# First batch of an attention and feed-forward kernel: two difference buffers and 512-wide exponentials in the key phases, one unit of 256 for the last 64 query tokens of four head pairs

## The chip, the core and the metric

The kernel runs on one core of a Trainium2 chip. The core has five engines with instruction queues of their own: TensorE (PE in the profile; its weight loads are shown apart as PEld), VectorE (DVE), ScalarE (ACT), GpSimd (POOL) and SyncE (SP, which issues the DMAs here). Each engine works its queue in order; semaphores tie the queues together. The metric is the time of one execution on the device in microseconds, and the median of several runs is compared. Less is better.

## The reference

Linear attention over 8 batches of 8 heads and 576 tokens, with a feature map of 2 x 128 exponentials, and then one feed-forward layer over all 4608 tokens:

```python
def phi(x):
    proj = np.einsum('bhsd,df->bhsf', x, w_phi)
    proj = proj - np.max(np.abs(proj), axis=-1, keepdims=True)
    return np.concatenate([np.exp(proj), np.exp(-proj)], axis=-1)
q_p, k_p = (phi(q), phi(k))
kv = np.einsum('bhsf,bhsd->bhfd', k_p, v)
z = np.sum(k_p, axis=2)
num = np.einsum('bhsf,bhfd->bhsd', q_p, kv)
den = np.einsum('bhsf,bhf->bhs', q_p, z)[..., None] + 1e-06
attn = num / den
x = attn.transpose(0, 2, 1, 3).reshape(4608, 512)
h = x @ w_in                      # 512 -> 2048
out = np.maximum(0.01 * h, h) @ w_out   # 2048 -> 512
```

## The kernel before

**Tiling.** Two heads share the 128 partitions, so a batch is four *pairs*; pairs 0 to 31 are worked in order, and pairs 0 to 3 are the first batch. The attention output of two batches at a time lies in `ring` (128 x 2 x 4 x 576): batch b writes half b mod 2. The feed-forward part works on 18 *blocks* of 256 tokens. Block 0 and block 1 lie within batch 0; block 2 has tokens 512 to 767, so it needs batch 0's last 64 tokens and also all four pairs of batch 1 (pairs 4 to 7). A block has 16 steps: `layer1(i, ft)` is 12 matmuls of 256 columns (L552, L553, L555), `layer2(i, ft)` 6 matmuls of 512 columns (L572 to L574), which follow three steps behind. Most products are split: a value is rounded to a shorter format (the cast, `copy_`, L67 on ACT, L69 on DVE), the rest is the difference (`tt_`, L72), and three matmuls make one product.

**Weights.** `load_weights` prepares 32 tiles (16 of `w_in`, 16 of `w_out`, in turns). Each is loaded by SP (L153) into one of two places in `ring[:, 1]`, the half that batch 1 will need later, and then takes on DVE L159, L160, L161, L164 and the difference of L72, on ACT L158, L163 and the cast of L67. Here `ql` and `kvl` are the names of its scratch tiles.

**The first batch.** It has its own code, since no feed-forward work is there yet to lie beside it. `first_k_phase(i)` makes the key side of pair i: three groups (128, 128 and 64 partitions) of projections (`proj`, three matmuls each), per group an absolute maximum (L417), a difference `pm` (L419, always the buffer `pmk`), then exponentials of `pm` and of `-pm` (L428, L429), 256 wide, two for each 128 tokens, and two matmuls into `kvp` (L431). At the end `kvp` is copied to `kvs`, transposed and stored as `kvh`. Phases 0 and 1 run together, step by step in turns, then 2 and 3. Odd phases take other buffers than even ones, some of them parts of `f2`, `f3`, `fr1`, `fr4`: four tiles whose space the last quarter of the weights takes over later (tag `late`). `first_q_phase(u)` makes the query side of all four pairs for the tokens of one unit: unit 0 has 256, unit 1 has 256, unit 2 has 64. Per pair: projections, L477 (maximum), L479 (difference `pmk`), transposes on PE, two exponentials (L492, L493) into `eq` or `qs`, matmuls with `kvh` (L500) into `nm`, copies of numerator and denominator (L502, L503), then L506 (transpose), L508 (reciprocal), L509 (transpose) on DVE and the product into `ring`.

**The later pairs** go through the generators `k_phase` and `q_phase`, which `attention` advances in turns: the keys of pair i beside the queries of pair i - 1. In `q_phase` the projections are L319 and L320, with L321 on DVE behind each; L338 and L343 prepare the exponentials, and L358 is the matmul with `kvh`. In `k_phase` L231 are key projections and L211 the matmuls into `kvp`.

**What sets the order.** The program is recorded with priorities, and a list scheduler with a timeline model of its own decides, once and at compile time, the order of the instructions on each engine: the first batch up to unit 0 before all, units 1 and 2 next, then later attention, then weights, then the feed-forward part. So a change to the first batch can move instructions of all later parts, and what is printed below as the order is what the engines work through.

```python
PF = -10 ** 6      # first batch, key phases and unit 0
PU = -600000       # units 1 and 2
PA = -500000       # later attention
PW = -250000       # weights; the feed-forward part has 0
```

Of the kernel before, what the change touches and what calls it, by code (L numbers as in the profile page):

```python
# [17 lines left out]
P = 128  # L18
# [26 lines left out]
def attention_moe_kernel(ctx: ExitStack, tc: tile.TileContext, q, k, v, vt, w_phi, w_in, w_out, out):  # L45
# [8 lines left out]
    def st(shape, dt, tag):  # L54
        return sp.tile(shape, dt, tag=tag, name=tag, bufs=BUFS.get(tag, 1))
# [47 lines left out]
    def part(x, i, shape):  # L103
        n = shape[0] * (shape[1] if len(shape) == 2 else 1)
        x = x[:, i : i + n]
        return x if len(shape) == 1 else x.rearrange("p (a b) -> p a b", b=shape[1])
# [281 lines left out]
    def first_k_phase(i):  # L388
# [18 lines left out]
        for g in range(3):  # L407
            pk = pt("a" if od else "acc")
            w = 2 if g < 2 else 1
            for s in range(w):  # L410
                t0 = (2 * g + s) * P if g < 2 else S - P
                proj(pk, s, kh[:, t0 : t0 + P], kl[:, t0 : t0 + P])
            r = slice(0, P) if g < 2 else slice(64, P)
            n = P if g < 2 else 64
            m4 = st([P, 4], F32, "m4")
            pkv = pk[r, 0 : 256 * w].rearrange("p (a f) -> p a f", f=F)
            nc.vector.tensor_reduce(m4[r, 0 : 2 * w], pkv, axis=AX.X, op=ALU.max, apply_absolute_value=True)  # L417
            pm = st([P, 4, F], F32, "pmk")
            nc.vector.tensor_tensor(pm[r, 0 : 2 * w], pkv,  # L419
                                    m4[r, 0 : 2 * w].unsqueeze(2).broadcast_to([n, 2 * w, F]), op=ALU.subtract)  # L420
            yield
            for s in range(w):
                c = 2 * g + s
                if c % 2:
                    ek = part(f2, 1236, [2, 256]) if od else st([P, 2, 256], F32, "kpl")
                else:
                    ek = st([P, 2, 256], F32, "kph" if od else "ek")
                nc.scalar.activation(ek[r, :, 0:F], pm[r, 2 * s : 2 * s + 2], AF.Exp)  # L428
                nc.scalar.activation(ek[r, :, F:256], pm[r, 2 * s : 2 * s + 2], AF.Exp, scale=-1.0)  # L429
                for j in range(2):  # L430
                    nc.tensor.matmul(kvp[0:66, 256 * j : 256 * j + 256], lhsT=rv[r, 4 * j + c if c < 4 else 8 + j], rhs=ek[r, j],  # L431
                                     start=c == 0 and j == 0, stop=c == 4, skip_group_check=True)
                yield
        kvs = st([P, 2, 256], F32, "kph" if od else "ek").rearrange("p a (b f) -> p a b f", b=2)[0:66]
# [12 lines left out]
        yield  # L447

# [13 lines left out]
    def first_q_phase(u):  # L462
        t0, w = units[u]
        rq, qh, ql = first_q[u]
        for hp in range(NP):
            copy_("qh", qh[:, hp], rq[:, hp])
            tt_("ql", ql[:, hp], rq[:, hp], qh[:, hp].bitcast(F32), ALU.subtract)
        yield
        for hp in range(NP):
            ns = max(1, w // P)  # L470
            n = min(P, w)
# [6 lines left out]
            pm = st([P, 4, F], F32, "pmk")  # L478
# [16 lines left out]
            kvh = kvs_of[hp][0]  # L495
            nm = pt("c" if u else "h")[:, 0 : 2 * w].rearrange("p (j t) -> p j t", j=2)
            dn = st([P, U], F32, "dn")[:, 0:w]
            for j in range(2):
                for t in range(2):
                    nc.tensor.matmul(nm[:, j], lhsT=kvh[:, j, t], rhs=ee[t][:, j], start=t == 0, stop=t == 1)  # L500
                rr = slice(64 * j, 64 * j + 64)
                nc.scalar.copy(ring[rr, 0, hp, t0 : t0 + w], nm[0:64, j])  # L502
                nc.scalar.activation(dn[rr], nm[64:128, j], AF.Copy, bias=1e-6)  # L503
# [6 lines left out]
            x = ring[:, 0, hp, t0 : t0 + w]  # L510
            tt_("x", x, x, dt, ALU.mult)
# [147 lines left out]
```

## Time and profile before

| | |
|---|---|
| median of 3 runs | 1270.08 us (1269.72 to 1270.16) |
| the profiled execution | 1268.76 us, span 1267.0 us |
| DMA | 57.03 MB, mean 45 GB/s |
| first batch and weight tiles, 0 to 169.4 us: DVE busy | 64.17 + 40.58 + 48.46 us |

The span runs from the first to the last recorded instruction; the execution's time has 1.76 us more around it. PE works for nearly the whole span, and its idle time lies in the first quarter, where the first batch and the weights are prepared. A row of a group names its line, engine, operation and tiles (written <- read), then the shapes, the count, the busy time and the mean in ns, and the idle time of the engine just before. A row of the timeline begins with its start and its length in us, and its bracket names the idle time before it and the instruction that ended it. A row of the table by stretches has the bounds, the length, then busy time and count for PE, PEld, DVE, ACT and POOL, the granted TensorE clock, the share of the DMA engines and the GB/s.

### The profile page before, as it was taken

To read this page: it belongs to the slowest core of one execution; us is meant where nothing else is said; L and a number is where in the kernel's file an instruction comes from. 1 tells how busy PE (TensorE), PEld (TensorE's weight loads), DVE (VectorE), ACT (ScalarE), POOL (GpSimd) and SP (SyncE) were. 2 spreads that over 40 slices of the span, in tenths; PEclk is the share of its full clock that TensorE was granted. 3 is DMA by queue.
4 is the path that set the end of the run, shared out by engine and by line. 5 is a ranking of instruction groups with operands and counts; after the bars stand their busy time and mean duration, and the time that the engine had idled before them with its cause. 6 is when DMAs were issued, how large, how long until landed. Compare 5 with 4: busy or idle time off the path is not lost. (4 is left out here: it accounts for less than half of the span.)

```text
span 1267.0 us, 21420 instructions
## 1 busy us (share of the span) xinstructions
PE 1189.0 (94%) x7564; PEld 1040.4 (82%) x7564; DVE 861.9 (68%) x1397; ACT 811.2 (64%) x2078; POOL 690.7 (55%) x720
## 2 busy tenths in 40 slices
PE   6679799879999999999999999999999999999998
PEld 5468688658888888889888889889988889999997
DVE  6999965677877888888978888824888788300000
ACT  6797765566676777777776767744777667433232
POOL 1234222336767767676767676744676767433232
PEclk9799999879999999999999999999999999999999
DMA  7434411211011111111111111110111010000000
GB/s 219 124 114 133 136 40 30 66 30 30 11 46 31 46 30 47 30 47 30 46 31 38 31 38 39 31 37 27 30 38 33 16 38 2 17 18 1 18 18 18
DMA packets 62780, 57.03 MB, mean 45 GB/s; under 512 B 45136, under 2 KB 46288, under 8 KB 62672
## 3 DMA queue, kind: packets, MB, share of 16 engines
q1 hardware_dynamic: 62672, 55.65, 15.6%
q8 instruction: 60, 0.98, 0.3%
q14 instruction: 48, 0.39, 0.1%
HBM read 46.20 MB, written 9.44 MB: 44 GB/s over the span
## 5 line engine op out<-in xcount | busy, mean ns | idle before, releaser
L72 POOL TENSOR_TENSOR gl<-g,gh 128x256 fp32r<-128x256 f32 x288 | 245.1, 855 | 287.4 <-ACT gh L67 213.4
L552 PE MATMUL h<-xh,w0h 128*128 128x256 f32 x1152 | 295.7, 284 | 3.8 <-ACT w0h L67 1.6
L553 PE MATMUL h<-xh,w0l 128*128 128x256 f32 x1152 | 295.1, 283 | 0.6 <-DVE w0l L72 0.6
L572 PE MATMUL acc<-w1h,gh 128*128 128x512 f32 x576 | 228.9, 398 | 2.9 <-DVE o L69 2.0
L552 PEld LDWEIGHTS h<-xh,w0h 128*128 128x128 f32 x1152 | 218.0, 189 | 16.0 <-ACT dn L503 2.1
L573 PE MATMUL acc<-w1l,gh 128*128 128x512 f32 x576 | 227.9, 396 | 0.0
L553 PEld LDWEIGHTS h<-xh,w0l 128*128 128x128 f32 x1152 | 217.9, 189 | 11.2 <-DVE w0l L72 1.0
L574 PE MATMUL acc<-w1h,gl 128*128 128x512 f32 x576 | 219.5, 397 | 2.3 <-POOL gl L72 2.3
L555 PE MATMUL h<-xl,w0h 128*128 128x256 f32 x1152 | 203.6, 284 | 0.7 <-POOL xl L72 0.6
L559 ACT ACTIVATE g<-h 128x256 f32<-128x256 f32 x288 | 108.6, 382 | 125.1 <-PE h L555 85.2
L72 POOL TENSOR_TENSOR ql<-eq,qh 128x576 fp32r<-128x576 f32 x96 | 154.9, 1622 | 52.2 <-DVE qh L69 41.1
L555 PEld LDWEIGHTS h<-xl,w0h 128*128 128x128 f32 x1152 | 166.0, 189 | 3.6 <-POOL xl L72 1.3
L67 ACT CAST gh<-g 128x256 fp32r<-128x256 f32 x288 | 115.2, 404 | 71.1 <-PE acc L573 66.2
L72 POOL TENSOR_TENSOR kpl<-ek,kph 128x512 fp32r<-128x512 f32 x72 | 105.0, 1458 | 50.3 <-ACT kph L67 30.6
L574 PEld LDWEIGHTS acc<-w1h,gl 128*128 128x128 f32 x576 | 106.2, 188 | 21.4 <-POOL gl L72 3.5
L572 PEld LDWEIGHTS acc<-w1h,gh 128*128 128x128 f32 x576 | 108.2, 188 | 17.5 <-DVE o L69 3.1
L573 PEld LDWEIGHTS acc<-w1l,gh 128*128 128x128 f32 x576 | 108.5, 188 | 12.8 <-DVE w1l L72 0.2
L69 DVE CAST qh<-eq 128x576 fp32r<-128x576 f32 x96 | 92.2, 967 | 33.6 <-ACT eq L344 25.7
L69 DVE COPY o<-acc 128x512 f32<-128x512 f32 x17 | 11.6, 682 | 132.6 <-DMA out_dram<-o 127.4
L343 ACT ACTIVATE eq<-mb 128x288 f32<-128x288 f32 x112 | 49.2, 439 | 78.6 <-DVE mb L338 71.8
L249 ACT ACTIVATE ek<-pmk 128x256 f32<-128x256 f32 (+1 forms) x128 | 53.4, 417 | 66.9 <-POOL kpl L72 25.3
L72 POOL TENSOR_TENSOR ring<-ring,mb 128x576 f32<-128x576 f32 (+2 forms) x40 | 51.4, 1285 | 56.8 <-DVE mb L372 24.7
(200 smaller groups left out, 2516.2 us busy)
## 6 DMA issues: line engine op xcount, KB each, us to landing
out_dram<-o SPq DMA_DIRECT2D x35, 256.0 KB, 2.0
rk<-in_k_dram SPq DMA_DIRECT2D x30, 288.0 KB, 2.9
ring<-in_w_in_dram SPq DMA_DIRECT2D x16, 512.0 KB, 3.6
ring<-in_w_out_dram SPq DMA_DIRECT2D x16, 512.0 KB, 3.6
rq<-in_q_dram SPq DMA_DIRECT2D x28, 288.0 KB, 2.8
rv<-in_v_dram SPq DMA_DIRECT2D x30, 256.0 KB, 3.4
rv<-in_vt_dram SPq DMA_DIRECT2D x60, 32.0 KB, 2.9
f<-in_k_dram SPq DMA_DIRECT2D x2, 288.0 KB, 4.2
```

Of the source, the lines that this page charges most:

```text
L67: nc.scalar.copy(o, i)
L69: (nc.vector if e == "v" else nc.gpsimd).tensor_copy(o, i)
L72: (nc.vector if pick(key) == "v" else nc.gpsimd).tensor_tensor(o, a, b, op=op)
L249: nc.scalar.activation(ek[r, :, 0:F], pmk[r, 2 * s : 2 * s + 2], AF.Exp)
L343: nc.scalar.activation(eq[:, 0], mb[:, u], AF.Exp)
L552: nc.tensor.matmul(ph, lhsT=weight(0, "h", ft)[:, d * P : d * P + P], rhs=xh[:, d], start=d == 0, stop=False)
L553: nc.tensor.matmul(ph, lhsT=weight(0, "l", ft)[:, d * P : d * P + P], rhs=xh[:, d], start=False, stop=False)
L555: nc.tensor.matmul(ph, lhsT=weight(0, "h", ft)[:, d * P : d * P + P], rhs=xl[:, d], start=False, stop=d == NP - 1)
L559: nc.scalar.activation(g, ph, AF.Prelu, alpha=0.01)
L572: nc.tensor.matmul(a, lhsT=gh[:, ts], rhs=weight(1, "h", ft), start=ft == 0, stop=False)
L573: nc.tensor.matmul(a, lhsT=gh[:, ts], rhs=weight(1, "l", ft), start=False, stop=False)
L574: nc.tensor.matmul(a, lhsT=gl[:, ts], rhs=weight(1, "h", ft), start=False, stop=ft == NFT - 1)
```

## The change

Three things are changed, all in the first batch.

In `first_k_phase` the difference `pm` no longer always takes the buffer `pmk`: an even phase takes `pmk` and `ek` in turns, an odd phase `kph` and `kpl`. Each group has one pair of exponentials 512 wide (256 wide for the group of 64 partitions) in place of one pair for each 128 tokens. They go to three buffers in turns for all phases together, `exps`: two are the halves of `ring[:, 0]` (its first 2048 elements), the third is `f3[1024:2048]`, into which unit 1's queries are loaded later. `kvs` always takes `kph`.

In `first_q_phase` all four pairs of a unit are cast by one instruction on DVE, where casts of 256 columns were, and their differences are two instructions. `pm` takes `pmk` and `ek` in turns. Unit 2, 64 tokens of four pairs, is treated as one unit of 256 tokens: 6 projection matmuls in place of 12, one maximum, one difference, four transposes on PE, one reciprocal with its two transposes; the matmuls with `kvh` are still made pair by pair, 16 of 64 columns, and the copies into `ring` have a stride.

```diff
@@ -415,23 +415,22 @@
             m4 = st([P, 4], F32, "m4")
             pkv = pk[r, 0 : 256 * w].rearrange("p (a f) -> p a f", f=F)
             nc.vector.tensor_reduce(m4[r, 0 : 2 * w], pkv, axis=AX.X, op=ALU.max, apply_absolute_value=True)
-            pm = st([P, 4, F], F32, "pmk")
+            pm = st([P, 4, F], F32, ("kpl" if g % 2 else "kph") if od else ("ek" if g % 2 else "pmk"))
             nc.vector.tensor_tensor(pm[r, 0 : 2 * w], pkv,
                                     m4[r, 0 : 2 * w].unsqueeze(2).broadcast_to([n, 2 * w, F]), op=ALU.subtract)
             yield
+            first_k["e"] = ne = first_k.get("e", -1) + 1
+            e = exps[ne % 3].rearrange("p (a t f) -> p a t f", t=2, f=F)
+            nc.scalar.activation(e[r, 0 : 2 * w, 0], pm[r, 0 : 2 * w], AF.Exp)
+            nc.scalar.activation(e[r, 0 : 2 * w, 1], pm[r, 0 : 2 * w], AF.Exp, scale=-1.0)
             for s in range(w):
                 c = 2 * g + s
-                if c % 2:
-                    ek = part(f2, 1236, [2, 256]) if od else st([P, 2, 256], F32, "kpl")
-                else:
-                    ek = st([P, 2, 256], F32, "kph" if od else "ek")
-                nc.scalar.activation(ek[r, :, 0:F], pm[r, 2 * s : 2 * s + 2], AF.Exp)
-                nc.scalar.activation(ek[r, :, F:256], pm[r, 2 * s : 2 * s + 2], AF.Exp, scale=-1.0)
                 for j in range(2):
-                    nc.tensor.matmul(kvp[0:66, 256 * j : 256 * j + 256], lhsT=rv[r, 4 * j + c if c < 4 else 8 + j], rhs=ek[r, j],
+                    nc.tensor.matmul(kvp[0:66, 256 * j : 256 * j + 256], lhsT=rv[r, 4 * j + c if c < 4 else 8 + j],
+                                     rhs=e[r, 2 * s + j].rearrange("p t f -> p (t f)"),
                                      start=c == 0 and j == 0, stop=c == 4, skip_group_check=True)
                 yield
-        kvs = st([P, 2, 256], F32, "kph" if od else "ek").rearrange("p a (b f) -> p a b f", b=2)[0:66]
+        kvs = st([P, 2, 256], F32, "kph").rearrange("p a (b f) -> p a b f", b=2)[0:66]
         copy_("kvs", kvs, kvp[0:66].rearrange("p (a b f) -> p a b f", a=2, b=2))
         kvt = pt("c")
         kvtv = kvt[:, 0:264].rearrange("p (a b f) -> p a b f", a=2, b=2)
@@ -446,6 +445,9 @@
             first_load_v(3)
         yield
 
+    r0 = ring[:, 0].rearrange("p a s -> p (a s)")
+    exps = [part(r0, 0, [1024]), part(r0, 1024, [1024]), part(f3, 1024, [1024])]
+
     units = [(0, 256), (256, 256), (512, 64)]
 
     def first_load_q(u):
@@ -462,20 +464,23 @@
     def first_q_phase(u):
         t0, w = units[u]
         rq, qh, ql = first_q[u]
-        for hp in range(NP):
-            copy_("qh", qh[:, hp], rq[:, hp])
-            tt_("ql", ql[:, hp], rq[:, hp], qh[:, hp].bitcast(F32), ALU.subtract)
-        yield
-        for hp in range(NP):
-            ns = max(1, w // P)
-            n = min(P, w)
+        nc.vector.tensor_copy(qh, rq)
+        for hp in range(0, NP, 2):
+            tt_("ql", ql[:, hp : hp + 2], rq[:, hp : hp + 2], qh[:, hp : hp + 2].bitcast(F32), ALU.subtract)
+        yield
+        tail = u == 2
+        if tail:
+            qh, ql = (x.rearrange("p a t -> p (a t)").unsqueeze(1) for x in (qh, ql))
+            w = NP * w
+        n, ns = P, 2
+        for hp in range(1 if tail else NP):
             pq = pt("a" if u else "acc")
             for s in range(ns):
                 proj(pq, s, qh[:, hp, s * P : s * P + n], ql[:, hp, s * P : s * P + n], n)
             m4 = st([P, 4], F32, "m4")
             pqv = pq[0:n, 0 : 256 * ns].rearrange("p (a f) -> p a f", f=F)
             nc.vector.tensor_reduce(m4[0:n, 0 : 2 * ns], pqv, axis=AX.X, op=ALU.max, apply_absolute_value=True)
-            pm = st([P, 4, F], F32, "pmk")
+            pm = st([P, 4, F], F32, "ek" if hp % 2 else "pmk")
             nc.vector.tensor_tensor(pm[0:n, 0 : 2 * ns], pqv,
                                     m4[0:n, 0 : 2 * ns].unsqueeze(2).broadcast_to([n, 2 * ns, F]), op=ALU.subtract)
             yield
@@ -492,14 +497,22 @@
             nc.scalar.activation(ee[0], tr, AF.Exp)
             nc.scalar.activation(ee[1], tr, AF.Exp, scale=-1.0)
             yield
-            kvh = kvs_of[hp][0]
             nm = pt("c" if u else "h")[:, 0 : 2 * w].rearrange("p (j t) -> p j t", j=2)
             dn = st([P, U], F32, "dn")[:, 0:w]
+            x = ring[:, 0, :, t0:S] if tail else ring[:, 0, hp : hp + 1, t0 : t0 + w]
+            m = x.shape[1]
+
+            def heads(y):
+                return y.rearrange("p (a t) -> p a t", a=m)
+
             for j in range(2):
-                for t in range(2):
-                    nc.tensor.matmul(nm[:, j], lhsT=kvh[:, j, t], rhs=ee[t][:, j], start=t == 0, stop=t == 1)
+                for h in range(m):
+                    ts = slice(w // m * h, w // m * h + w // m)
+                    for t in range(2):
+                        nc.tensor.matmul(nm[:, j, ts], lhsT=kvs_of[hp + h][0][:, j, t], rhs=ee[t][:, j, ts],
+                                         start=t == 0, stop=t == 1)
                 rr = slice(64 * j, 64 * j + 64)
-                nc.scalar.copy(ring[rr, 0, hp, t0 : t0 + w], nm[0:64, j])
+                nc.scalar.copy(x[rr], heads(nm[0:64, j]))
                 nc.scalar.activation(dn[rr], nm[64:128, j], AF.Copy, bias=1e-6)
             yield
             dt = st([P, U], F32, "mb")[:, 0:w]
@@ -507,8 +520,7 @@
             rc = st([P, 9], F32, "rc")[:, 0 : w // 32]
             nc.vector.reciprocal(rc, dt.rearrange("p (a c) -> p a c", c=32)[:, :, 0])
             nc.vector.transpose(dt.rearrange("p (a c) -> p a c", c=32), rc.unsqueeze(2).broadcast_to([P, w // 32, 32]))
-            x = ring[:, 0, hp, t0 : t0 + w]
-            tt_("x", x, x, dt, ALU.mult)
+            tt_("x", x, x, heads(dt), ALU.mult)
             yield
 
     end = object()
```

The order on the engines moves with it. The first place is PE around the last query projection of pair 7 (L319 and L320 with `qs`); L231 and L211 with `ks`, `kph`, `kpl` are the key side of pair 8, `xh` and `xl` are the split tokens of a block, `w0h` and `w0l` a weight tile of the first layer, `w1h` and `w1l` one of the second, and L358 is the first matmul of pair 7's exponentials. Before:

```order
L319 MATMUL a<-qs,wq 128x288
L320 MATMUL a<-qs,wq 128x288
L231 MATMUL a<-wq,ks 128x256 x4
L552 MATMUL h<-xh,w0h_836 128x256
L553 MATMUL h<-xh,w0l_837 128x256
...
L211 MATMUL c<-kph,vh 66x256
L211 MATMUL c<-kph,vl 64x256
...
L358 MATMUL a<-eq,kvh 128x288
```

And of the changed kernel, whose lines are 12 higher there (L564, L565 and L567 are the first layer, L584 to L586 the second):

```order
L319 MATMUL a<-qs,wq 128x288
L320 MATMUL a<-qs,wq 128x288
L564 MATMUL h<-xh,w0h_991 128x256
L565 MATMUL h<-xh,w0l_992 128x256
...
L231 MATMUL a<-wq,ks 128x256 x2
L567 MATMUL h<-xl,w0h_991 128x256 x4
...
L584 MATMUL acc<-w1h_1004,gh 128x512
L585 MATMUL acc<-w1l_1005,gh 128x512
L586 MATMUL acc<-w1h_1004,gl 128x512
...
L211 MATMUL c<-kph,vh 66x256
```

Steps of both layers, which stood ahead of pair 7's last projection, now stand behind it, between it and pair 8's key matmuls; in the whole stretch up to the first matmul of block 2 that needs pair 7 there are 24 matmuls of the first layer and 24 of the second, where there were 4 and none.

The second place is DVE at the end of the key phases. L417 is the maximum of a group, L419 its difference; `m_352`, `m_360` (before) and `m_322`, `m_330` (changed) are the last groups of pairs 2 and 3, and L159, L160, L161, L164 and L72 belong to weight tiles. Before:

```order
L164 ISA ql<-ql,kvl 128x1024
L419 TENSOR_TENSOR pmk<-a,m_325 128x512
L159 TENSOR_SCALAR ql<-ql 128x512
L417 TENSOR_REDUCE m_360<-a 64x2
L72 TENSOR_TENSOR w0l_837<-ql,w0h_836 128x512
L160 TENSOR_SCALAR ql<-ql 128x512
L161 SCALAR_TENSOR_TENSOR ql<-ring,ql 128x512
L419 TENSOR_TENSOR pmk<-acc,m_352 64x256
```

And of the changed kernel:

```order
L419 TENSOR_TENSOR kph<-a,m_268 128x512
L419 TENSOR_TENSOR kpl<-a,m_302 128x512
L160 TENSOR_SCALAR ql<-ql 128x512
L417 TENSOR_REDUCE m_322<-acc 64x2
L417 TENSOR_REDUCE m_330<-a 64x2
L161 SCALAR_TENSOR_TENSOR ql<-ring,ql 128x512
L72 TENSOR_TENSOR w1l_729<-ql,w1h_728 128x512
L419 TENSOR_TENSOR pmk<-acc,m_322 64x256
L164 ISA ql<-ql,kvl 128x1024
L419 TENSOR_TENSOR kph<-a,m_330 64x256
```

The maxima and differences stand closer together, and fewer weight tiles are between them: one tile has one L164, and the last L417 of the key phases stands behind 5 of them before and behind 2 now. Further on, the first maximum of pair 4 (L239, now L239 too) stands behind 22 tiles before and behind 13 now.

The third place is SP, ahead of the weights. `f_79` is `f2`, with pair 3's keys and values, `f_80` is `f3`, into which unit 1's queries go, and `ring` is the stage of the weight tiles. Before:

```order
L117 DMA rk<-in_k_dram 128x576
L117 DMA f_79<-in_k_dram 128x576
L123 DMA f_79<-in_vt_dram 64x2x64
L459 DMA f_80<-in_q_dram 128x4x256
L459 DMA rq<-in_q_dram 128x4x64
L153 DMA ring<-in_w_in_dram 128x1024
L153 DMA ring<-in_w_out_dram 128x1024
```

And of the changed kernel, from the sixth weight tile on:

```order
L153 DMA ring<-in_w_out_dram 128x1024
L153 DMA ring<-in_w_in_dram 128x1024
L461 DMA f_80<-in_q_dram 128x4x256
L153 DMA ring<-in_w_out_dram 128x1024
L176 DMA rv<-in_v_dram 128x8x64
L177 DMA rv<-in_vt_dram 64x2x64
L178 DMA rv<-in_vt_dram 64x2x64
```

The load of unit 1's queries, which stood ahead of the first weight tile, now stands behind the seventh, and the eighth tile and pair 4's values (`rv`) stand behind it.

## The prediction

> **What bounds the kernel now.** The page comes first: its span, the share of TensorE (PE), and the two slice rows for PE and its granted clock.
>
> ```profile
> span 1267.0 us, 21420 instructions
> PE 1189.0 (94%) x7564; PEld 1040.4 (82%) x7564; DVE 861.9 (68%) x1397; ACT 811.2 (64%) x2078; POOL 690.7 (55%) x720
> PE   6679799879999999999999999999999999999998
> PEclk9799999879999999999999999999999999999999
> ```
>
> PE is busy 1189.0 of 1267.0 us, so all but 78 us is matmul work that has to be done in any order, and the end of the kernel is the sum of that work and of PE's idle time. The slices say that the idle time lies early. The second view is the table by stretches. I cut them where the work changes: first feed-forward matmul at 75.6, first reduction of pair 4 on DVE at about 118, last weight tile split at 169.4, last query projection of pair 7 at 243.4, first matmul that needs pair 7's result at 272.7.
>
> ```profile
> 0.00:75.60 75.60, 51.67 (x242) 37.17 (x242) 64.17 (x121) 54.77 (x122) 17.40 (x31) 0.86 0.56 163
> 75.60:118.00 42.40, 38.74 (x246) 33.67 (x247) 40.58 (x81) 35.31 (x80) 18.64 (x16) 1.00 0.43 125
> 118.00:169.40 51.40, 43.44 (x259) 34.76 (x257) 48.46 (x93) 40.02 (x102) 16.00 (x20) 1.00 0.43 118
> 169.40:243.40 74.00, 73.13 (x432) 62.13 (x430) 35.30 (x67) 45.49 (x123) 19.98 (x30) 1.00 0.15 41
> 243.40:272.70 29.30, 17.18 (x65) 11.42 (x64) 22.90 (x39) 16.78 (x41) 8.64 (x8) 0.72 0.10 30
> 272.70:840.00 567.30, 547.95 (x3633) 487.61 (x3632) 468.72 (x717) 402.02 (x1042) 393.42 (x375) 1.00 0.13 36
> 840.00:1267.00 427.00, 416.93 (x2695) 373.65 (x2694) 181.75 (x285) 216.79 (x572) 216.62 (x241) 1.00 0.07 21
> ```
>
> Columns after the length: busy time of PE, PEld, DVE, ACT, POOL, then the granted clock. Three things are to be seen. Up to 169.4 VectorE (DVE) is nearly full (48.46 of 51.40 in the third row): it prepares 32 weight tiles and does the first batch's attention. From 169.4 to 243.4 PE is full (73.13 of 74.00). Then comes a **gap** of 29.3 us in which PE works 17.18 us at a clock of 0.72: it has run out of token blocks 0 and 1, and block 2 needs the second batch. The chain that fills the gap, from the last projection of pair 7 to the first dependent matmul of block 2:
>
> ```profile
> 243.28 0.29 PE L320 MATMUL a<-qs,wq 128*128 128x288 f32 x1
> ...
> 269.24 1.40 POOL L72 TENSOR_TENSOR ring<-ring,mb 128x576 f32<-128x576 f32 x1 [0.86 <-ACT ek L250]
> ...
> 272.75 0.41 PE L552 MATMUL h<-xh,w0h 128*128 128x256 f32 x1
> ```
>
> And PE's waits in the stretch from 240 to 275, longest first:
>
> ```profile
> PE a L358 <- ACT eq L343: 3.6, 2, 2.3
> PE c L211 <- ACT kph L67: 3.0, 2, 2.3
> PE a L319 <- DVE tq L321: 2.8, 3, 1.3
> ```
>
> PE waits there for the steps of pair 7 (and of pair 8, which stands between them), not for data or weights. From 272.7 on PE is at 96 to 98%, and what comes later is not touched by the change except through the shift.
>
> **The change part by part.** *1. The order at the gap* is the main term. I counted the feed-forward matmuls in the rows of the order from pair 7's last projection to the first matmul of block 2 that needs pair 7. Before has 4 of the first layer (0.33 of a step of 12) and none of the second; after has 24 (2.00 steps) and 4 steps of 6 of the second. The price of a step is read from three starts in the full stretch:
>
> ```profile
> 188.57 0.28 PE L552 MATMUL h<-xh,w0h 128*128 128x256 f32 x1
> ...
> 190.00 0.40 PE L572 MATMUL acc<-w1h,gh 128*128 128x512 f32 x1
> ...
> 191.39 0.28 PE L552 MATMUL h<-xh,w0h 128*128 128x256 f32 x1
> ```
>
> A first-layer step is 1.43 us, a second-layer step 1.39 us. So 1.67 x 1.43 + 4 x 1.39 = 7.9 us of matmuls move from ahead of the projection into the gap, where PE is idle 29.3 - 17.18 = 12.1 us. The projection comes 7.9 us earlier; if the gap keeps its 29.3 us, block 2 starts 7.9 us earlier. Why attention is ahead is the two difference buffers: the K phases of pairs 0 to 3 end after 2 weight tiles on DVE instead of after 5. Bounds: 0, if the chain before the projection is late by as much as PE has less to do, and 7.9 plus the gap's lost clock, 17.18 x 0.28 = 4.8, together 12.7. I take 7.9, since the stretch ahead of it (73.13 of 74.00) is full of matmuls and shortens with their number.
>
> *2. The last 64 tokens as one unit.* On DVE four units of 64 tokens become one of 256. Rows of the groups from 0 to 200 us, the small forms first:
>
> ```profile
> L477 DVE TENSOR_REDUCE m<-a 64x2 f32<-64x256 f32 x4 | 1.6, 407 | 0.0
> L479 DVE TENSOR_TENSOR pmk<-a,m 64x256 f32<-64x256 f32 x4 | 1.6, 408 | 0.0
> L506 DVE STREAM_TRANSPOSE mb<-dn 128x64 f32<-128x64 f32 x4 | 0.9, 237 | 0.7 <-ACT dn L503 0.7
> L509 DVE STREAM_TRANSPOSE mb<-rc 128x64 f32<-128x64 f32 x4 | 1.0, 242 | 0.1
> L477 DVE TENSOR_REDUCE m<-a 128x4 f32<-128x512 f32 x4 | 2.6, 662 | 0.0
> L479 DVE TENSOR_TENSOR pmk<-a,m 128x512 f32<-128x512 f32 x4 | 2.7, 678 | 0.0
> L506 DVE STREAM_TRANSPOSE mb<-dn 128x256 f32<-128x256 f32 x8 | 3.5, 435 | 0.4 <-ACT dn L503 0.3
> L509 DVE STREAM_TRANSPOSE mb<-rc 128x256 f32<-128x256 f32 x8 | 3.5, 433 | 0.0
> ```
>
> Four times (0.407 + 0.408 + 0.237 + 0.242) is 5.2 us; once (0.662 + 0.678 + 0.435 + 0.433) is 2.2: 3.0 us less. PE loses 6 of the unit's 12 projection matmuls, 6 x 0.12 = 0.7 us by the step above; the rest stays (16 matmuls of 64 columns as before).
>
> *3. The casts.* Four casts of a unit become one:
>
> ```profile
> 12.05 0.89 DVE L69 CAST xh<-qs 128x256 fp32r<-128x256 f32 x4
> 49.15 1.96 DVE L69 CAST fr<-f 128x256 fp32r<-128x256 f32 x4
> ```
>
> The elements stay, so the gain is between 0 and, should the second take what the first takes, 1.96 - 0.89 = 1.1 us. The one that I take, 0, keeps the elements.
>
> Of these 3.0 to 4.1 us of DVE, between none and all reach the end: none, if the matmuls of block 0 are not what DVE holds up, all, if DVE's last weight tile is. The third stretch has both, PE idle 8.0 us with DVE at 94%, so I take 2.
>
> *4. 512-wide exponentials.* Pitch of two 256-wide, and of two 512-wide ones that exist already:
>
> ```profile
> 30.57 0.41 ACT L429 ACTIVATE ek<-pmk 128x256 f32<-128x256 f32 x1
> 30.88 0.40 ACT L428 ACTIVATE kpl<-pmk 128x256 f32<-128x256 f32 x1
> 57.60 0.59 ACT L492 ACTIVATE eq<-a 128x512 f32<-128x512 f32 x1
> 58.08 0.60 ACT L493 ACTIVATE eq<-a 128x512 f32<-128x512 f32 x1
> ```
>
> 0.31 against 0.48, eight against four in each of four phases: 4 x (8 x 0.31 - 4 x 0.48) = 2.2 us of ACT. ACT is not full anywhere before 169 (40.02 of 51.40), and each pair of matmuls now waits for two wider exponentials: between 0 and 2.2, I take 0, hidden under DVE. If DVE had room, the 2.2 would count.
>
> *5. The query load of unit 1 waits.* Its place in SP's queue moves from ahead of all weight tiles to behind the seventh, since the third exponential buffer lies in its target. It waits for the last matmul that reads it; the eighth weight tile and the values of pair 4 queue behind it.
>
> ```profile
> 46.57 1.08 PE L431 MATMUL h<-kph,f 64*66 64x256 f32 x4 [1.12 <-ACT kph L429]
> 53.36 0.33 SPq L153 DMA_DIRECT2D ring<-in_w_out_dram  x1
> ...
> rq<-in_q_dram SPq DMA_DIRECT2D x28, 288.0 KB, 2.8
> ```
>
> Even where the last K matmul ended at 47.65 as before, the eighth tile, issued at 53.36, would not be held. The cast itself starts at 49.15 and needs the load landed: between 0 and 1.3 us (47.65 plus the 2.8 us to landing that the page gives for query loads, less 49.15). The K phase now ends sooner, so 0.
>
> **Sum.** 7.9 + 0.7 + 2 = 10.6 us. The profiled execution took 1268.76 us (span 1267.0 and 1.76 around it): 1258.2. The median of the runs is 1.3 above it: 1259.5. The bounds add up to a gain of 0 to 12.7 + 0.7 + 4.1 = 17.5, that is 1252.6 to 1270.1 (with 4 and 5 at their ends some 2 us further either way).
>
> **The rivals.** *A. Only the removed work counts.* The moved matmuls meet a chain that is late by as much: 0.7 + 2 = 2.7 us, 1267.4. For it: the order is planned ahead and a queue in fixed order waits where the plan was off, as in the gap. Against it: PE is full for 74 us ahead of the gap, so fewer matmuls there mean an earlier projection.
>
> *B. The gap also gets its clock back.* With 25 us of matmuls in 29.3, PE might keep the full clock: 4.8 us more, 1254.7. For it: every stretch with PE over 84% busy has clock 1.00. Against it: the chain's steps on ACT, DVE and POOL set the gap's length as much as PE's pace does. [...]
>
> *C. Slower: PE stalls under full DVE.* Pair 4 starts after 13 weight tiles on DVE instead of 22, so the mixture of second-batch attention and weight tiles, which in before runs from 118 to 169.4 with PE idle 7.96 of 51.4 (0.155), now reaches back to about 75.6, and PE's queue is in order: a projection or a key matmul that waits for DVE holds the feed-forward matmuls behind it. In before the 93.8 us from 75.6 to 169.4 have 11.6 us of idle time (0.124). The gap shows 0.413 as the worst share. Half way between 0.155 and 0.413, 0.284, is 26.6 us, 15 more: 1259.5 + 15 = 1274.5. It turns the change slower by 0.2% from a share of (11.6 + 10.6 + 2.5) / 93.8 = 0.263 on. Against it: 0.155 itself adds only 2.9 us, and the weight tiles hold up those matmuls there anyway.
>
> *D. It does nothing:* a later stretch gives it all back, 1270.1. Against it: from 272.7 on PE's idle time is 2 to 4%, and the order of the last 2600 PE rows is the old one.
>
> **How the numbers follow.** Forecast 0.50 (own range 1255 to 1264), A 0.16, B 0.16, C 0.12, D 0.06. The range takes in the forecast, A and B: 1252 to 1268; C and D stay out with 0.18. About 0.2% (2.5 us) is what a measurement of this kernel can tell from no change. A lies on that edge and is halved: faster 0.50 + 0.16 + 0.08 = 0.74, within 0.2% 0.08 + 0.06 = 0.14, slower 0.12.
>
> **What would show it.** Step 1: the first dependent matmul of block 2 near 262, PE busy some 25 us in the 29 us ahead of it; were the gap as idle as now, step 1 is wrong. Clock 1.00 there would be B. Step 2: the four DVE groups of 64 tokens gone, one of 256, and the last weight tile split before 169. PE idle above 25 us between 75 and 169 would be C. Step 5: a cast of unit 1 that waits for its load would show its price. The prediction is wrong altogether if the stretch behind block 2 is longer than the 994.3 us (1267.0 - 272.7) that it has now.

## The result, and the profile after

The changed kernel takes 1242.35 us in the median (five runs; 1241.55 the lowest) against 1270.08 before; the ratio is 0.9776, with an interval of 0.9764 to 0.9788. It is 27.7 us faster; 10.6 were forecast, and the range ended at 1252. One of the five executions, the profiled one, took 1885.11 us at a TensorE clock of 0.557; the profile used here is that of a repeat, which took 1243.06 (four runs, ratio 0.9787, 0.9771 to 0.9803) and is called "changed" below.

The page of the changed kernel, in the lines that were shown of before: the span, the busy times by engine, and the slices of PE and of its clock.

```profile
span 1240.5 us, 21324 instructions
PE 1181.5 (95%) x7554; PEld 1039.1 (84%) x7554; DVE 861.3 (69%) x1373; ACT 806.7 (65%) x2044; POOL 686.8 (55%) x711
PE   6889799989999999999999999999999999999998
PEclk9999899989999999999999999999999999999999
```

The span is 26.5 us shorter, PE is busy 7.5 us less, so 19 us of its idle time have gone. Not all of it lay early, as the slices of before suggest: of the 78 us before, 29.4 lie behind the first matmul of block 2 that needs pair 7 (994.25 us long, PE busy 964.83). DVE is busy as long as before (861.3 against 861.9), although it has 24 instructions fewer. To see where the time went, the stretches are cut at the same events as before: first feed-forward matmul, last difference of a weight tile on DVE, last query projection of pair 7, first matmul of block 2 that needs pair 7. Timeline rows of the last three in the changed kernel, and of the weight tile's in the kernel before:

```profile
166.29 0.65 DVE L72 TENSOR_TENSOR w1l<-ql,w1h 128x512 fp32r<-128x512 f32 x1
227.71 0.30 PE L320 MATMUL a<-qs,wq 128*128 128x288 f32 x1
255.23 0.41 PE L564 MATMUL h<-xh,w0h 128*128 128x256 f32 x1
...
168.17 1.24 DVE L72 TENSOR_TENSOR w1l<-ql,w1h 128x512 fp32r<-128x512 f32 x1
```

The table by stretches of the changed kernel (columns as before: length, then busy time and count of PE, PEld, DVE, ACT, POOL, the clock):

```profile
0.00:65.03 65.03, 48.74 (x253) 34.98 (x253) 56.19 (x102) 48.66 (x100) 16.96 (x26) 0.95 0.59 167
65.03:166.29 101.26, 88.05 (x497) 71.54 (x498) 95.70 (x176) 82.91 (x185) 25.69 (x31) 0.95 0.44 127
166.29:227.71 61.42, 61.42 (x373) 52.62 (x373) 34.46 (x64) 37.98 (x101) 18.43 (x24) 1.00 0.17 45
227.71:255.23 27.52, 22.56 (x117) 17.85 (x116) 21.15 (x37) 20.40 (x54) 13.53 (x16) 0.89 0.13 41
255.23:850.50 595.27, 580.79 (x3860) 521.87 (x3860) 477.52 (x725) 414.46 (x1081) 411.53 (x400) 0.99 0.13 35
850.50:1240.50 390.00, 379.95 (x2461) 340.25 (x2459) 176.29 (x273) 202.25 (x529) 200.71 (x217) 1.00 0.07 22
166.29:255.23 88.94, 83.98 (x488) 70.47 (x488) 55.62 (x101) 58.38 (x154) 31.96 (x40) 0.97 0.16 44
```

And of the kernel before, cut at the last weight tile as well:

```profile
0.00:168.17 168.17, 132.61 (x739) 104.57 (x740) 151.98 (x292) 128.97 (x299) 50.81 (x66) 0.94 0.49 141
168.17:272.75 104.58, 91.59 (x504) 74.63 (x502) 59.48 (x106) 63.40 (x167) 29.85 (x39) 0.92 0.13 37
272.75:876.86 604.11, 584.76 (x3867) 520.86 (x3866) 474.50 (x729) 416.53 (x1084) 409.20 (x400) 1.00 0.13 34
876.86:1267.00 390.14, 380.07 (x2461) 340.35 (x2459) 175.92 (x273) 202.28 (x529) 200.84 (x217) 1.00 0.07 22
```

The span is three lengths, and they account for all of it. The last weight tile is done 1.9 us earlier (168.17 to 166.29). From there to the matmul that needs pair 7 it is 15.6 us shorter (104.58 to 88.94): PE has 8.0 us less idle time in it (12.99 to 4.96) and 7.6 us less to do. Behind it 9.0 us go: 8.8 (604.11 to 595.27) up to the end of block 10, 0.1 after it. The sum is 26.5. That the first feed-forward matmul comes 10.6 us earlier (75.63 to 65.03) is not in this sum: the work that PE does sooner waits for the weights all the same.

Most of the 7.6 us less to do are attention of pair 4. Group of the products of exponentials and `kvh` in the middle length, before and changed:

```profile
L358 PE MATMUL a<-eq,kvh 128*128 128x288 f32 x64 | 20.7, 437 | 3.6 <-ACT eq L343 3.6
...
L358 PE MATMUL a<-eq,kvh 128*128 128x288 f32 x48 | 14.0, 408 | 1.7 <-ACT eq L343 1.7
```

Before has four pairs (16 records each) left when the weights are done, changed has three: pair 4's products now lie ahead of the last weight tile, where PE has idle time in any case (13.2 of 101.26 us). Up to pair 7's last projection the group falls by 16 records, from 14.2 to 9.2 us, and twelve smaller matmuls (L319, L320, L379 to L381) leave with them. The other 1.7 us between the two rows is no work that left: the 16 records of the gap, the stretch behind that projection, stay 16 and took 4.8 us instead of 6.5, at a clock of 0.89 instead of 0.72. Pair 4's first maximum on DVE had moved from 118.85 to 78.20:

```profile
118.85 0.68 DVE L239 TENSOR_REDUCE m<-a 128x4 f32<-128x512 f32 x1
...
78.20 0.64 DVE L239 TENSOR_REDUCE m<-a 128x4 f32<-128x512 f32 x1
```

### The profile page after: what moved, and what is told of

It is laid out like the page before. It is cut to its first block, busy times and chain, and to the rows that moved or that the text cites. A ratio compares the mean times of both kernels' runs of the same rounds, so it can differ in the third digit from the quotient of the medians.

```text
span 1883.3 us, 21324 instructions
## 1 busy us (share of the span) xinstructions
PE 1864.4 (99%) x7554; PEld 1474.4 (78%) x7554; DVE 776.5 (41%) x1373; ACT 825.9 (44%) x2044; POOL 638.6 (34%) x711
## 4 chain that ended last, share of the span: by engine, by line
PE 98%; ACT 1%; DMA 1%; DVE 1%; issue 0%; ACTq 0%; DVEq 0%
PE h L564 12%; PE acc L585 12%; PE acc L584 12%; PE h L567 12%; PE h L565 12%; PE acc L586 12%; PE c L211 9%; PE a L358 3%; PE a L231 2%; PE a L363 2%; PE a L360 2%; PE h L429 2%; PE a L319 1%; PE a L320 1%; PE c L512 1%; PE c L281 1%
## 5 line engine op out<-in xcount | busy, mean ns | idle before, releaser
L72 POOL TENSOR_TENSOR gl<-g,gh 128x256 fp32r<-128x256 f32 x288 | 222.7, 774 | 699.8 <-ACT gh L67 535.6
L564 PE MATMUL h<-xh,w0h 128*128 128x256 f32 x1152 | 430.6, 386 | 2.1 <-ACT g L571 1.2
L565 PE MATMUL h<-xh,w0l 128*128 128x256 f32 x1152 | 428.8, 384 | 0.0
L584 PE MATMUL acc<-w1h,gh 128*128 128x512 f32 x576 | 333.3, 579 | 1.7 <-ACT gh L67 1.6
L585 PE MATMUL acc<-w1l,gh 128*128 128x512 f32 x576 | 334.2, 580 | 0.0
L586 PE MATMUL acc<-w1h,gl 128*128 128x512 f32 x576 | 322.5, 579 | 0.0
L565 PEld LDWEIGHTS h<-xh,w0l 128*128 128x128 f32 x1152 | 277.5, 241 | 40.7 <-issue 20.0
L564 PEld LDWEIGHTS h<-xh,w0h 128*128 128x128 f32 x1152 | 272.8, 237 | 42.9 <-issue 16.0
L567 PE MATMUL h<-xl,w0h 128*128 128x256 f32 x1152 | 300.7, 385 | 0.0
L567 PEld LDWEIGHTS h<-xl,w0h 128*128 128x128 f32 x1152 | 251.5, 266 | 6.6 <-issue 1.7
L584 PEld LDWEIGHTS acc<-w1h,gh 128*128 128x128 f32 x576 | 137.6, 239 | 49.7 <-issue 26.1
L586 PEld LDWEIGHTS acc<-w1h,gl 128*128 128x128 f32 x576 | 127.7, 225 | 60.3 <-issue 24.4
L72 POOL TENSOR_TENSOR ql<-eq,qh 128x576 fp32r<-128x576 f32 x96 | 140.4, 1469 | 88.3 <-PE a L363 72.9
L72 POOL TENSOR_TENSOR kpl<-ek,kph 128x512 fp32r<-128x512 f32 x72 | 98.3, 1365 | 163.9 <-PE c L211 106.9
L321 DVE STREAM_TRANSPOSE tq<-a 128x288 f32<-128x288 f32 x112 | 52.8, 475 | 142.2 <-PE a L320 141.8
```

The source lines that it names most:

```text
L72: (nc.vector if pick(key) == "v" else nc.gpsimd).tensor_tensor(o, a, b, op=op)
L564: nc.tensor.matmul(ph, lhsT=weight(0, "h", ft)[:, d * P : d * P + P], rhs=xh[:, d], start=d == 0, stop=False)
L565: nc.tensor.matmul(ph, lhsT=weight(0, "l", ft)[:, d * P : d * P + P], rhs=xh[:, d], start=False, stop=False)
L567: nc.tensor.matmul(ph, lhsT=weight(0, "h", ft)[:, d * P : d * P + P], rhs=xl[:, d], start=False, stop=d == NP - 1)
L584: nc.tensor.matmul(a, lhsT=gh[:, ts], rhs=weight(1, "h", ft), start=ft == 0, stop=False)
L585: nc.tensor.matmul(a, lhsT=gh[:, ts], rhs=weight(1, "l", ft), start=False, stop=False)
```

## The experiments

Every kernel below was profiled, and its span cut in the same three lengths: to the last weight tile's difference on DVE, from there to the first matmul of block 2 that needs pair 7, and the rest. "Behind" is the number of feed-forward matmuls of the first and second layer that its order has between pair 7's last projection and that matmul. Orders behind block 2 that agree in their last 6240 or more PE rows have one letter; a trace has 7554 or 7564, of which 6314 to 6327 lie behind that matmul. Lengths and span are those of one profiled execution each; the ten executions of one kernel (before, other priority) took 1266.15 to 1273.52 us, so a difference of 2 or 3 us between two rows is not shown to be the kernels'. The table comes first, since the runs are read against each other; medians in us, ratios to the kernel before on the same chip.

| kernel | behind | order | lengths, us | span | median | ratio (interval) |
|---|---|---|---|---|---|---|
| before | 4 + 0 | A | 168.2 + 104.6 + 994.3 | 1267.0 | 1270.08 | 1 |
| casts only | 4 + 0 | A | 171.2 + 104.6 + 995.5 | 1271.3 | 1270.89 | 1.001 (0.9997 to 1.0022) |
| before, other priority | 4 + 0 | D | 171.2 + 105.0 + 991.5 | 1267.6 | 1267.84 | 0.9986 (0.9971 to 1.0001) |
| wide only | 4 + 0 | own | 165.9 + 101.8 + 994.7 | 1262.4 | 1264.23 | 0.996 (0.9945 to 0.9975) |
| tail and two buffers | 12 + 16 | A | 168.4 + 96.0 + 996.4 | 1260.7 | 1261.07 | 0.993 (0.9911 to 0.9949) |
| changed, narrow | 12 + 16 | D | 166.5 + 95.1 + 994.2 | 1255.8 | 1256.56 | 0.9898 (0.988 to 0.9917) |
| tail only | 12 + 21 | own | 168.1 + 91.8 + 980.5 | 1240.4 | 1243.99 | 0.9799 (0.9784 to 0.9815) |
| changed, four small units | 12 + 18 | own | 169.0 + 88.7 + 987.9 | 1245.6 | 1247.82 | 0.9827 (0.9807 to 0.9847) |
| key part | 24 + 24 | B | 177.3 + 88.5 + 986.4 | 1252.2 | 1252.86 | 0.9861 (0.984 to 0.9882) |
| query part | 24 + 24 | B | 172.3 + 87.0 + 984.4 | 1243.8 | 1248.04 | 0.9828 (0.9808 to 0.9847) |
| changed | 24 + 24 | B | 166.3 + 88.9 + 985.3 | 1240.5 | 1243.06 | 0.9787 (0.9771 to 0.9803) |
| narrow, other priority | 24 + 24 | B | 168.6 + 88.9 + 985.0 | 1242.5 | 1243.44 | 0.9785 (0.9763 to 0.9806) |
| narrow, other buffer | 24 + 24 | B | 170.4 + 88.8 + 986.3 | 1245.6 | 1247.20 | 0.9814 (0.9789 to 0.9839) |
| two buffers only | 24 + 24 | C | 172.0 + 88.4 + 980.4 | 1240.7 | 1243.11 | 0.9797 (0.978 to 0.9813) |
| changed, other priority | 24 + 24 | C | 165.5 + 88.1 + 981.3 | 1235.0 | 1236.56 | 0.9737 (0.9722 to 0.9753) |

**The halves of the change.** Two theories stood against each other: "order", that the place of the instructions brings the time, and "work", that the instructions taken away do. First the changed kernel again:

> The changed kernel itself, for a trace of it at full clock. Theory 'order': pair 7's last query projection comes earlier by 8 us or more and the stretch between it and the first matmul of block 2 that needs pair 7 still has about 29 us, now with 25 us of PE work in it; median 1242 as before. Theory 'work': the last weight tile is split 15 to 25 us earlier than 169 and everything behind it is only shifted; the idle time of PE goes from the first 169 us, not from the gap. Rival 'clock': the gap keeps its length in work and the clock in it goes from 0.72 to 1.00 (at most 4.8 us).

Its readings are above: pair 7's last projection is 15.6 us earlier, the last weight tile only 1.9, and the gap has 22.6 us of PE work in 27.5. Then the first half, `first_k_phase` of the change with `first_q_phase` of before, and the second, the other way round:

> The key phases of the change alone, with the query phases of before (casts by pair, one difference buffer, four units of 64). Its order at pair 7's last projection is that of the changed kernel (24 and 24 matmuls behind it). 'Order': 1243 to 1248, nearly the whole gain. 'Work': about half of the gain, 1253 to 1260, since the query phases' work on DVE is as before.

> The query phases of the change alone, with the key phases of before (one difference buffer, 256-wide exponentials). Its order at pair 7's last projection is again that of the changed kernel. 'Order': 1243 to 1248. 'Work': 1253 to 1260; and this run's gain and that of the key part add up to about 27.7 us.

The key part gained 16.8 us (1252.86 against the 1269.64 of the kernel before beside it), the query part 21.6; together 38.4, where the whole change has 26.6. So they don't add up, which speaks against "work". The query part lies at the upper edge of the bracket of "order"; the key part fell between the two brackets, only 0.1 us below that of "work", since its last weight tile came at 177.3 instead of 168.2, 9.2 us late. Its middle length is that of the changed kernel, as its order is. Then the merged unit was taken out again:

```diff
-        tail = u == 2
+        tail = False
 ...
-        n, ns = P, 2
+        n, ns = min(P, w), max(1, w // P)
```

> The changed kernel with unit 2 again as four units of 64 tokens. Its order has 12 first-layer and 18 second-layer matmuls behind pair 7's last projection, 5.6 us by the price of a step, against 8.4 for the changed kernel. 'Order': 2 to 4 us slower than the changed kernel, 1244 to 1246. 'Work': slower by the 3.0 us of DVE and 0.7 of PE as well as the ACT and waits of four small units, 1246 to 1252.

It was 4.8 us slower, 1247.82, which is in the bracket of "work". Its lengths say that only part of that is work: the last weight tile is 2.7 us later, about the 3.0 us of DVE that the forecast gave the unit, but another 2.6 us lie behind block 2, where it has an order of its own. The middle length, 88.7, is the changed kernel's, though only 12 and 18 feed-forward matmuls stand behind the projection: PE works 81.5 us in it, not 84.0, and idles 7.1, not 5.0. So the count "behind" does not set the middle length by itself.

**One edit each, on the kernel before.** The merged unit 2 alone; two difference buffers alone (with the three exponential buffers, but 256-wide); 512-wide exponentials with one difference buffer; casts alone. Two buffers alone (+) and wide alone (-) differ in two places:

```diff
-            pm = st([P, 4, F], F32, "pmk")
+            pm = st([P, 4, F], F32, ("kpl" if g % 2 else "kph") if od else ("ek" if g % 2 else "pmk"))
 ...
-            nc.scalar.activation(e[r, 0 : 2 * w, 0], pm[r, 0 : 2 * w], AF.Exp)
-            nc.scalar.activation(e[r, 0 : 2 * w, 1], pm[r, 0 : 2 * w], AF.Exp, scale=-1.0)
             for s in range(w):
                 c = 2 * g + s
+                nc.scalar.activation(e[r, 2 * s : 2 * s + 2, 0], pm[r, 2 * s : 2 * s + 2], AF.Exp)
+                nc.scalar.activation(e[r, 2 * s : 2 * s + 2, 1], pm[r, 2 * s : 2 * s + 2], AF.Exp, scale=-1.0)
```

> The kernel before with one edit: unit 2 as one unit of 256. It removes 3.0 us of DVE and 0.7 us of PE, and its order has 12 first-layer matmuls and 3.5 second-layer steps behind pair 7's last projection, 6.3 us by the price of a step (before: 0.5). 'Order': PE idle in the gap about 6 us instead of 12, and 1250 to 1256. 'Work' (only what is removed counts): 1264 to 1268.

> The key part with its two difference buffers for each phase and three exponential buffers, but 256-wide exponentials as before, and the query phases of before. Its order at pair 7's last projection is that of the changed kernel (24 and 24 matmuls behind it). 'Order': 1250 to 1257, within 4 us of the whole key part (1252.9). 'Width' (the 512-wide exponentials bring the key part's gain): 1262 or more.

> The key part with 512-wide exponentials but the one difference buffer of before, and the query phases of before. Its order at pair 7's last projection is that of before (4 and 0 matmuls behind it). 'Order': the gap has 12 us of idle PE as before, and 1262 to 1270. 'Width': 1250 to 1257.

> The kernel before with one edit: the casts of a unit as one instruction and their differences as two. The order of feed-forward and attention matmuls from pair 4 on is that of before. 'Order' and 'work' both: 1267 to 1270, at most the 1 us that the longer cast might save on DVE. More than 3 us would mean that the first batch's chain waits for these casts.

The two edits that move the order gained the whole of it, each by itself (1243.99 and 1243.11, both below the bracket of "order"), the two that don't stayed near the kernel before (1264.23 and 1270.89). Three more expectations were missed. Casts alone lay 0.9 us above their bracket, with a ratio that has one in its interval. The gap of wide alone had 8.3 us of idle time, not 12, and wide alone still gained 5.9 us, 2.2 of it at the last weight tile. And two buffers alone were to lie within 4 us of the key part, which is the same edit with 512-wide exponentials: that one is 9.8 us slower, with its last weight tile 5.4 us later and order B, 6.0 us longer, in place of C. All kernels with 4 + 0 have the products of four pairs left when the weights are done (60 to 64 records of the group shown above), all others those of three (48). The clearest is two buffers alone. The line of busy times from its page and its three lengths:

```profile
PE 1182.6 (95%) x7564; PEld 1037.2 (84%) x7564; DVE 857.3 (69%) x1397; ACT 810.1 (65%) x2078; POOL 691.2 (56%) x720
...
171.96:260.31 88.35, 83.49 (x486) 69.39 (x486) 55.04 (x100) 57.86 (x153) 31.97 (x40) 0.98 0.16 44
260.31:1240.70 980.39, 959.48 (x6321) 859.03 (x6320) 649.34 (x999) 617.73 (x1610) 613.84 (x616) 1.00 0.11 30
```

The counts of instructions are those of before on all engines (7564, 1397, 2078, 720), so no instruction was saved. The last weight tile comes 3.8 us later than before, and the span is still 26.3 us shorter: 16.2 in the middle length, 13.9 behind it. Wide alone, with the order of before at pair 7, keeps a long middle length and the full length behind it:

```profile
165.93:267.70 101.77, 93.50 (x527) 77.12 (x525) 58.69 (x109) 66.01 (x171) 32.89 (x43) 0.93 0.14 39
267.70:1262.40 994.70, 963.24 (x6314) 862.04 (x6314) 656.99 (x996) 615.38 (x1606) 610.73 (x614) 1.00 0.11 30
```

**Is the length behind block 2 the order's, or does it follow from an earlier second batch?** Four kernels whose order behind block 2 is that of another: merged unit 2 and two buffers together (256-wide exponentials, old casts), whose last rows are those of before; the changed kernel and the kernel before with one number changed; and the changed kernel with 256-wide exponentials.

```diff
-PA = -500000
+PA = -700000
```

> The kernel before with the merged unit 2 and the two difference buffers, but 256-wide exponentials and the casts of before: both edits that gained 26 us alone. Its PE order at pair 7's last projection has 12 first-layer matmuls and 16 second-layer ones behind it, 5.1 us (before 0.5), but its last 6347 PE rows, all from block 2's start on, are those of before. 'Later order' (the order behind block 2 has a price of its own, whatever came before): the stretch behind block 2's first dependent matmul takes 994 to 996 us as in before, and the median is 1247 to 1255, slower than either edit alone. 'State' (that stretch is shorter because the second batch is done earlier): 975 to 986 us, and 1235 to 1243.

> The changed kernel with the priority of the later attention set ahead of units 1 and 2: the same work, ordered otherwise. Its last 6818 PE rows are those of the two-buffers run, which took 980.4 us behind block 2's first dependent matmul (the changed kernel: 985.3). 'Later order': 979 to 982 us there and a median of 1236 to 1240. 'State': 985 and 1242 to 1244.

> The kernel before with the same shift of priority: not one instruction more or less. At pair 7's last projection its order is that of before (4 and 0 matmuls behind it), behind block 2 its last 6347 PE rows are those of the next run. 'Later order': up to block 2 as before, 271 to 277 us; behind it the same time as the next run, within 2 us. 'State': 994 us behind it, 1267 to 1272 in all.

> The changed kernel with 256-wide exponentials. In its order 12 first-layer and 16 second-layer matmuls stand behind pair 7's last projection. 'Later order': behind block 2 the same time as the run before, within 2 us, wherever between 975 and 995 that is. 'State': 975 to 986, while the run before has 994. 'Width': the first feed-forward matmul comes later than the changed kernel's 65.0 us, by up to 2.

The last stretch of the four, in that order:

```profile
264.35:1260.70 996.35, 966.64 (x6326) 862.60 (x6325) 649.57 (x1002) 619.05 (x1612) 611.08 (x616) 1.00 0.11 30
...
253.66:1235.00 981.34, 960.41 (x6321) 860.26 (x6320) 649.17 (x999) 617.59 (x1610) 614.84 (x616) 1.00 0.11 30
...
276.13:1267.60 991.47, 964.32 (x6326) 861.51 (x6325) 660.09 (x1002) 616.82 (x1612) 610.83 (x616) 1.00 0.11 30
...
261.56:1255.80 994.24, 966.23 (x6326) 862.60 (x6325) 662.92 (x1002) 616.88 (x1612) 610.47 (x616) 1.00 0.11 30
```

Two edits that had gained 26 us each gained 8.6 together, since the planner came out at the order of before behind block 2 (996.35; "state" had 975 to 986). Its total missed the bracket: the middle length was 96.0, not the changed kernel's 88.9. The changed kernel with the other priority has the last length of the two-buffers run, as expected (981.34 against 980.39), and is the fastest kernel here. The last pair agrees to 2.8 us, a little more than the 2 expected, with the second batch 14.6 us apart; "state" had 8 us or more between them. "Width" had the first feed-forward matmul of the narrow kernel later than the changed kernel's 65.03; it came at 63.91, earlier.

**Width or order?** What remained was 13.5 us between the changed kernel and its narrow variant, which differ in both. Two variants keep the narrow exponentials and come out at the changed kernel's order, one by the priority, one by the name of a buffer:

```diff
-        kvs = st([P, 2, 256], F32, "kph")
+        kvs = st([P, 2, 256], F32, "kph" if od else "ek")
```

> The changed kernel with 256-wide exponentials (which took 1256.6) and the priority of the later attention ahead of units 1 and 2. Same work as that run, other order: the last 6823 PE rows are those of the changed kernel, with 24 and 24 matmuls behind pair 7's last projection instead of 12 and 16. 'Order': 87 to 89 us from the last weight split to the first dependent matmul of block 2 (narrow: 95.1), 984 to 987 behind it (narrow: 994.2), and a median of 1240 to 1246. 'Width' (the narrow exponentials themselves cost the 13.5 us against the changed kernel): 1253 to 1259.

> The changed kernel with 256-wide exponentials, with the buffer of the key sums for even pairs as in the kernel before: no instruction differs from the narrow run. Its last 6823 PE rows are again those of the changed kernel. 'Order': as the run before, 1240 to 1246. 'Width': 1253 to 1259.

The first took 1243.44, the changed kernel's time. Its last two stretches:

```profile
168.58:257.48 88.90, 84.27 (x488) 69.95 (x488) 55.62 (x101) 58.35 (x154) 32.00 (x40) 0.97 0.16 44
257.48:1242.50 985.02, 959.24 (x6319) 859.89 (x6318) 654.56 (x998) 616.37 (x1609) 613.64 (x616) 1.00 0.11 30
```

Both lengths are the changed kernel's to 0.3 us. The second took 1247.20, 1.2 above the bracket: its lengths behind the weights are the same (88.8 and 986.3), the last weight tile is at 170.4. So at most some 4 us are left for anything but the order of PE, and that in the time of the last weight tile.

## Why the prediction was wrong

- **Step 1, the order at the gap:** the mechanism was right, the size was not. The matmuls moved into the gap as counted: PE works 22.56 us in it instead of 17.35, and from the last weight tile to the end of the gap its idle time falls by 8.0 us, where 7.9 were forecast. The other half was missed. The prediction took the length ahead of the projection as shortened only by the moved feed-forward matmuls; but pair 4's query products left it too, with smaller matmuls of its attention, for a stretch where PE idles, and the gap got part of its clock back; with both, PE has 7.6 us less to do up to the end of the gap. Pair 4's start after 13 weight tiles instead of 22 stood in the prediction, but only as a danger (rival C).
- **"What comes later is not touched by the change except through the shift":** this failed, and it is the largest single miss, 9.0 us. The prediction had compared the last 2600 PE rows, which are the same, and let that stand for all rows behind block 2; some 3700 rows between were ordered anew. PE had 29.4 us of idle time there, so there was room for another order to gain. Orders A, B, C and D have 994 to 996, 984 to 986, 980 to 981 and 991 to 994 us there, whatever came ahead.
- **Step 2, the merged unit:** taking it out again moved the last weight tile by 2.7 us, near the 3.0 us of DVE; but with the merged unit alone that tile came only 0.1 us earlier than before (168.06 against 168.17), so the price is not confirmed. That this edit, alone, gains 26 us is the order's doing.
- **Step 3, the casts at nothing:** right, 1.001 with one in the interval; nothing of the 0 to 1.1 us showed.
- **Step 4, the wide exponentials at nothing, at most 2.2:** right at the changed kernel's order. There narrow (with the other priority) and wide differ by 0.4 us in the median and by 2.3 at the last weight tile, just over that bound. Where the order moved with the width, wide was 13.5 us faster than narrow in the changed kernel and 5.9 faster alone, but 9.8 slower beside two buffers only.
- **Step 5, the late query load at nothing:** right. The load goes out at 41.64 and its cast on DVE starts at 46.85 with no wait for it.

```profile
41.64 0.38 SPq L461 DMA_DIRECT2D f<-in_q_dram  x1
...
46.85 0.69 DVE L467 CAST fr<-f 128x1024 fp32r<-128x1024 f32 x1
```

- **The 2 us of DVE:** the last weight tile came 1.9 us earlier, in size as forecast, but not for the reason given, so the size is luck. DVE works as long ahead of that tile as before (56.19 + 95.70 = 151.9 us, against 151.98), with attention of pair 4 in the place of what was removed; what fell is DVE's idle time, from 16.2 to 14.4 us.
- **Rival A** (a chain that is late by as much) falls with the projection 15.6 us earlier. **Rival B** came in part: the clock in the gap rose from 0.72 to 0.89, not to 1.00, and the low clock lasted on behind it: from 255.23 to 263.00 it is 0.50 although PE is busy for 6.67 of 7.77 us, and up to 261.51 its matmuls of 256 columns start about 0.21 us apart, where they start 0.12 apart at 1.00 (before: 0.51 from 272.75 to 276.80, with PE busy for all 4.05 us). So "every stretch with PE over 84% busy has clock 1.00", which spoke for B, does not hold in the changed kernel. PE's longest waits in the changed kernel from 225 to 257 us:

```profile
PE a L358 <- ACT eq L343: 1.7, 1, 1.7
PE c L211 <- DVE kph L269: 1.0, 1, 1.0
```

  Waits of up to 1.7 us came with a clock of 0.89 here, waits of up to 2.3 us with 0.72 in before; what lowers the clock is not shown by these runs.
- **Rival C** (PE stalls under full DVE): from the first feed-forward matmul to the last weight tile PE is idle 13.2 of 101.26 us, a share of 0.130, hardly more than the 0.124 it was held against, and far from the 0.263 at which it would decide. **Rival D** falls with the result.

What stays open: which feature of the order behind block 2 costs up to 16 us (980.4 to 996.4). About half of the difference between before and changed is PE's idle time there (29.4 to 24.5 us), the rest lies within its busy time (964.8 to 960.7 for 7 matmuls fewer); it is spread over many blocks, and no single wait carries it. Open too is why the last weight tile comes anywhere from 165.5 to 177.3 us: DVE works 149.3 to 156.1 us ahead of it and idles for the rest, 14.3 to 21.3.

## What to carry to other kernels

Where a planner fixes the order, an edit is priced by the order it comes out at, not only by its instructions: compare all the rows from the edit to the end, not the place that is expected to matter and the tail, and treat any stretch with new rows as unknown by one or two per cent (here up to 16 of 980 us). Find the event that late work waits for (here the last weight tile) and cut the span there: what moves ahead of it into idle time is gained (here 5.0 us of pair 4's products), and what is merely sooner ahead of it is not (here the first feed-forward matmul, 10.6 us). Before a gain is credited to an edit, run the edit with another order and the order with another edit; a name of a buffer or a priority is enough to do it.

## What had not been expected of the hardware

DVE's busy time hardly followed its instruction count: 24 instructions fewer took 861.3 against 861.9 us, while two buffers alone, with all 1397, took 857.3. In the changed kernel the clock stayed at 0.50 from 255.23 to 263.00, where PE was 86% busy. Kernels with the same order behind block 2 repeat that length within 3 us, so the 16 us between orders are no noise of the chip.
